# First batch's token mixing with the height tiles outermost, its weights decoded in pairs, and the second batch's attention written behind it

## The chip, the cores and the metric

One core of one Trainium2 chip. The metric is the device time of one execution in microseconds; the kernel before took 1106.73 us (median of 3 runs, 1104.41 to 1109.35). Engines: PE (TensorE, matrix products into eight PSUM banks), DVE (VectorE), ACT (ScalarE), POOL (GpSimd), SP (issues most of the DMAs, in order).

## The reference

Eight batches of 576 tokens and 512 channels go through linear attention and two mixer layers. Per batch:

```
kv  = k^T v per head;  x = rmsnorm(q kv) * g_norm        # 8 heads of 64
th  = x @ w_theta;  zr, zi = x*cos(th), x*sin(th)
y   = w_tok_r @ zr + w_tok_i @ zi                         # token mixing, 576 x 576 each
u   = x + y;  x2 = u + relu(u @ w_ch)                     # channel mixing
u2  = x2 + (relu(x2^T w_tok1) w_tok2)^T                   # second layer: tokens (256) ...
out = u2 + relu(u2 @ w_ch1) @ w_ch2                       # ... and channels (1536)
```

The mixer weights arrive as float64, so the kernel itself turns their two 32 bit words into float32 and those into a float16 pair.

## The kernel before

Each product of precision is made of three float16 matmuls (`mm3`): high by high, high by low, low by high. So every operand, weight or activation, exists as a pair of tiles, made by one ACT instruction (high) and one DVE instruction (low). A float64 weight tile costs more: ACT scales the upper word (L148), DVE shifts it (L154), ors in the lower word (L155) and the sign (L156), ACT makes the high half (L176), DVE the low one (L178).

A batch goes through these units, each a generator whose steps are run one by one:

- `kv` (L295): key by value sums, then the block diagonal `kvbd` (ACT L309, DVE L310), one buffer for all batches.
- `attend` r = 0 to 4 (L316): `po` = q by kvbd for 128 tokens (64 in the last), square (ACT L335), sum (DVE L337), inverse root (POOL L338, L339), x (DVE L342). Batch 0 transposes x on PE (`px`, L350; pair by L67, L68). Later batches make the pair xs (ACT L357, DVE L359) and transpose it by DMA (L360); R, the residual, follows (L363, L365).
- `rotate` r = 0 to 4: `pt` = the angles; L393 to L405 turn them into x cos and x sin (tile cs, two buffers), and L409, L412 write the pair zh, zl at the height tiles r and r + 4. The last one, r = 4 (64 tokens, cos and sin as one ninth height tile), works transposed and brings its tile zt to zh by a DMA transpose (L457). zt has the tag xs, which has two buffers, with batch 1's xs.
- `mix` (L462): for a chunk c of output tokens (256 or 320 columns) and a block dt of 128 channels, one accumulation over all nine height tiles kk in one PSUM bank; then the residual (DVE L483) and the pair u (ACT L484, DVE L487).
- `channel`, `token1`, `token2`: the layers that follow, with evictions at L509 to L517, L72 and L552.

Around them stands a planner: the code is written unit by unit, and the tile framework orders the instructions of each engine by the place where they are written and by when buffers and inputs are free in its own model of time. What is written later runs earlier where its inputs and buffers are there. Blocks marked `urgent` count as written 120 instructions earlier.

The start (L768 to L790) does kv and attend of batch 0, with a mixing weight tile after each (`spare`), then its rotations with the rest of those tiles, then loads batch 1's heads and does its kv. Nine raw weight tiles come by DMA into buffers that the z tiles will use: pairs of adjacent tiles in tag zh, single ones in tag zl, two buffers each. `prepare` names batch 0's own zh and zl; they get a buffer at their first write. Then the loop over b begins (L828): for b = 0 `run` does the eight mix blocks M00 to M13, each followed by a unit of batch 1 (a0 to a4, r0 to r2), then eight channel blocks with r3 and r4 and the w_tok weights; `l` loads a later batch's heads. For b = 1 the first four mix blocks are followed by token mixing of batch 0's second layer, beside which batch 2's attention starts.

PSUM is one pool of eight banks (`bank`), taken in turn by whatever is written.

Of the kernel before, what the change touches and what calls it, by code (L numbers as in the profile page):

```python
# [19 lines left out]
P = 128  # L20
# [8 lines left out]
def attn_mixer_kernel(  # L29
# [17 lines left out]
    HP = H // 2  # L47
    CHUNKS = ((0, 2 * P), (2 * P, S))
    NC = S // 2
    KH, MH, DH = KF // 2, KD // 2, KD // 2  # L50
    ps = ctx.enter_context(tc.tile_pool(name="ps", bufs=8, space=PSUM))
    dr = ctx.enter_context(tc.tile_pool(name="dr", bufs=1, space=DRAM))
# [23 lines left out]
    def lead(ins):  # L76

        last[ins.ins.engine] = ins.ins
        return ins
# [78 lines left out]
    def weight(pool, w, src, part, n, hi, lo, scale, name, raw=None):  # L158

        if pool is stg:  # L160
            val = pool.tile([P, n], F32, tag="val", name=f"{name}v")[:part]
        else:
            val = pool.tile([P, 8, P], F32, tag="st", name=f"{name}v").rearrange("p x n -> p (x n)")[:part, :n]
        if w.dtype == F32:
            load(val, src)
            yield
        else:
            if raw is None:
                raw = pool.tile([P, 4, P, 2] if pool is not stg else [P, n, 2], I32, tag="raw", name=f"{name}r")
                if pool is not stg:  # L170
                    raw = raw.rearrange("p a n w -> p (a n) w")
                raw = raw[:part, :n]
                load(raw.rearrange("p n w -> p (n w)"), src)
            yield
            yield from decode(val, raw)
        nc.scalar.activation(hi, val, AF.Copy, scale=scale)  # L176
        yield
        nc.vector.scalar_tensor_tensor(lo, val, scale, hi, ALU.mult, ALU.subtract)  # L178

    def words(w):  # L180
        return (w, 1) if w.dtype == F32 else (w.bitcast(I32), 2)

    def weight_tile(pool, w, pr, j, n, scale, name, col=0, raw=None):
        at = slice(col, col + n)
        src, k = words(w)
        src = src[j * P:(j + 1) * P, k * col:k * (col + n)]
        return weight(pool, w, src, P, n, pr[0][:, j, at], pr[1][:, j, at], scale, f"{name}{col}_{j}", raw)

    def mix_weights():

        if w_mix.dtype == F32:
            return [weight_tile(stg, w_mix, wm, j, S, SW, "wm") for j in range(KM)]
        units = []
        for j in range(KM):
            if j % 3 == 2:
                t, n = zp.tile([P, KM - 1, DM], F16, tag="zl", name=f"wmr{j}"), 1
            elif j % 3 == 0:
                t, n = zp.tile([P, KM + 1, DM], F16, tag="zh", name=f"wmr{j}"), 2
            else:
                continue  # L200
            t = t.rearrange("p a b -> p (a b)").bitcast(I32)[:, :n * 2 * S]
            src = w_mix.bitcast(I32)[j * P:(j + n) * P, :].rearrange("(k p) n -> p k n", p=P)
            nc.sync.dma_start(t.rearrange("p (k n) -> p k n", k=n), src)
            t = t.rearrange("p (k n w) -> p k n w", k=n, w=2)
            units += [weight_tile(stg, w_mix, wm, j + k, S, SW, "wm", raw=t[:, k]) for k in range(n)]
        return units


    wad = [dr.tile([P, KH, DH, 7, P], F16, name=f"wad{i}") for i in range(2)]
# [160 lines left out]
    def prepare(o):  # L370
        if o.zh is None:

            o.zh = zp.tile([P, KM + 1, DM], F16, tag="zh", name=f"zh{o.b}")
            o.zl = zp.tile([P, KM - 1, DM], F16, tag="zl", name=f"zl{o.b}")

    def rotate(o, r):

        b = o.b
        if r == 0:
            prepare(o)  # L380
        zh, zl, x, xt = o.zh, o.zl, o.x[r], o.xt[r]
        if r == NR:
            yield from rotate_last(o, xt)
            return
        pt = bank(f"pt{b}{r}")
        mm3(pt, [(xt[:, 0, kk, :], xt[:, 1, kk, :], wth[:, kk, :], wtl[:, kk, :]) for kk in range(KD)])

        cs = fp.tile([P, 2, DM], F32, tag="cs", name=f"cs{b}{r}", bufs=2)
        f, sn = cs[:, 0], cs[:, 1]
        place = beside(o)  # L390
        yield
        with early(o):
            place(nc.scalar.activation(f, pt, AF.Copy, bias=MAGIC))  # L393
        if b > 1:
            yield
        with early(o):
            place(nc.vector.scalar_tensor_tensor(f, f, MAGIC, pt, ALU.subtract, ALU.subtract))
        yield
        with early(o):
            place(nc.scalar.activation(sn, f, AF.Sin, scale=-RAD))  # L400
            nc.scalar.activation(f, f, AF.Abs)
            nc.scalar.activation(f, f, AF.Sin, bias=hpi, scale=-RAD)
        yield
        with early(o):
            place(nc.vector.tensor_tensor(cs, cs, x.unsqueeze(1).to_broadcast([P, 2, DM]), ALU.mult))  # L405
        yield
        at = slice(r, r + NR + 1, NR)
        with early(o):
            place(nc.scalar.activation(zh[:, at, :], cs, AF.Copy))  # L409
        yield  # L410
        with early(o):
            place(nc.vector.tensor_tensor(zl[:, at, :], cs, zh[:, at, :], ALU.subtract))  # L412

    def rotate_last(o, xt):


        b = o.b
        pt = bank(f"pt{b}{NR}")[:, :KD * SR].rearrange("p (k t) -> p k t", k=KD)
        for dt in range(KD):
            ds = slice(dt * P, (dt + 1) * P)  # L420
            mm3(pt[:, dt, :], [(wth[:, kk, ds], wtl[:, kk, ds], xt[:, 0, kk, :SR], xt[:, 1, kk, :SR]) for kk in range(KD)])
        cs = fp.tile([P, 2, DM], F32, tag="cs", name=f"cs{b}{NR}", bufs=2)
        f = cs[:, 0, :KD * SR].rearrange("p (k t) -> p k t", k=KD)
        sn = cs[:, 1, :].rearrange("p (k i t) -> p k i t", k=KD, i=2)
        zt = fp.tile([P, 2, DM], F16, tag="xs", name=f"zt{b}", bufs=2)
        place = beside(o)
        yield
        with early(o):
            place(nc.scalar.activation(f, pt, AF.Copy, bias=MAGIC))
        if b > 1:  # L430
            yield
        with early(o):
            place(nc.vector.scalar_tensor_tensor(f, f, MAGIC, pt, ALU.subtract, ALU.subtract))
        yield
        with early(o):
            place(nc.scalar.activation(sn[:, :, 1, :], f, AF.Sin, scale=-RAD))
            nc.scalar.activation(f, f, AF.Abs)
            nc.scalar.activation(sn[:, :, 0, :], f, AF.Sin, bias=hpi, scale=-RAD)
        if b > 1:
            yield  # L440
        R = o.R[:, :, SM:]
        with early(o):
            for i in range(2):
                place(nc.vector.scalar_tensor_tensor(sn[:, :, i, :], R, 1.0 / SW, sn[:, :, i, :], ALU.mult, ALU.mult))
            place(nc.scalar.activation(R, R, AF.Copy, scale=gn))
        yield
        sn = sn.rearrange("p k i t -> p (k i t)")
        with early(o):
            place(nc.scalar.activation(zt[:, 0, :], sn, AF.Copy))
        yield  # L450
        with early(o):
            place(nc.vector.tensor_tensor(zt[:, 1, :], sn, zt[:, 0, :], ALU.subtract))
        if b > 1:

            for _ in range(3):
                yield
        place(nc.sync.dma_start_transpose(  # L457
            o.zh[:, KM - 1:, :].rearrange("p i (k d) -> p (i k) d", k=KD), zt.rearrange("p i n -> p (i n)")
        ))


    def mix(o, c, dt):  # L462
# [22 lines left out]
        yield  # L485
        with urgent():
            lead(nc.vector.scalar_tensor_tensor(ul[:, dt, :], u, 1.0 / SW, uh[:, dt, :], ALU.mult, ALU.subtract))  # L487

    def channel(o, c, ct):
        b, R = o.b, o.R  # L490
# [249 lines left out]
    def go(unit, lead=False):  # L740
        advance()
        next(unit)
        (leading if lead else pending).append(unit)
# [16 lines left out]
    def spare(n=1):  # L760
        for _ in range(min(n, len(extra))):
            go(extra.pop(0))
# [10 lines left out]
    load_q(o, P)  # L773
    for part in range(2):
        go(kv(o, part))
    go(attend(o, 0))
    prepare(o)
    extra += mix_weights()
    for r in range(1, NR + 1):
        go(attend(o, r))  # L780
        spare()
    for r in range(NR + 1):
        go(rotate(o, r))
        if r > 1:
            spare()
    spare(len(extra))
    nxt = load_heads(1)
    for part in range(2):
        go(kv(nxt, part))
    flush()  # L790
    extra += [weight_tile(stg, w_ch, wc, j, DM, SW, "wc") for j in range(KD)]

# [35 lines left out]
    for b in range(B):  # L828
        loaded.clear()
        if b == 0:  # L830
            run(MIX, o, nxt, None, {
                "M00": "a0 w", "M01": "a1 w", "M02": "a2 w", "M03": "a3 w", "M10": "a4 r0 w", "M11": "r1 l w", "M12": "r2 w", "M13": "w",
            })
            after = loaded[0]
            spare(len(extra))
            flush()
# [5 lines left out]
            extra += [weight(wp[0], w_tok1, src[SM:], SR, DT, w1rh[:SR], w1rl[:SR], SW, "w1r")]  # L842
            extra += [weight_tile(wp[0], w_tok2, w2, j, S // 2, SW, "w2", col) for j in range(KJ) for col in range(0, S, S // 2)]
            run(CHANNEL, o, nxt, after, {
                "C00": "w", "C01": "r3 w", "C02": "w", "C03": "r4 w", "C10": "w", "C11": "w", "C12": "w", "C13": "w",
            })
            spare(len(extra))
            for t in (w1rh, w1rl):
# [95 lines left out]
```

## Time and profile before

| | |
|---|---|
| runs | 1104.41, 1106.73, 1109.35 us |
| profiled execution | 1103.0 us, its span 1101.2 us, granted clock 0.994 |
| busy over the span | PE 97%, DVE 74%, ACT 51%, POOL 17% |
| PE, tenths of the first four slices of 27.5 us | 4, 7, 7, 9 |
| DVE, the same | 4, 9, 8, 9 |
| granted PE clock, the same | 9, 9, 8, 9 |
| DMA in the first slice | 311 GB/s |
| chain that ended last | PE 86%, DVE 7%, DMA 3% |
| POOL inverse root (L339), mean of 40 | 1720 ns |
| ACT square (L335) and xs (L357), means | 583 and 622 ns |

Busy is the share of time in which an engine worked on something. A slice is one of 40 equal parts of the span, and its digit is in tenths. For an engine's cost per instruction the step from one start to the next is read where instructions stand back to back, since their durations overlap a little. Times in the rows are us from the start of the span.

### The profile page before, as it was taken

Reading aid. Unit: us, or ns where it says so; the run is one execution under the profiler, and the core shown is the slowest. Engines: PE = TensorE matmul, PEld = TensorE weight load, DVE = VectorE, ACT = ScalarE, POOL = GpSimd, SP = SyncE. Lnnn points to the kernel's source line nnn. Section 1 sums busy time; section 2 is a strip of 40 time slices with the busy share of each in tenths; the row PEclk is TensorE's granted clock in tenths of the full one; section 3 lists DMA queues with packets and bytes.
Section 4 is the critical chain, followed back from the end, with each engine's and each line's share of the span. In section 5 each row is a group of like instructions: output and inputs, shape, how many; then the busy total and the mean of one; then the engine's idle time right before and its main releaser. Section 6 shows DMA issues by size and latency. Waiting matters only on the chain.

```text
span 1101.2 us, 21603 instructions
## 1 busy us (share of the span) xinstructions
PE 1066.4 (97%) x8884; PEld 813.7 (74%) x8884; DVE 812.7 (74%) x1475; ACT 565.7 (51%) x966; POOL 186.7 (17%) x252
## 2 busy tenths in 40 slices
PE   4779999999999999999999999999999999999998
PEld 4466776767777678776877777777777777777776
DVE  4989868887988869877654685758586775758484
ACT  3857536556465654646431645446363645446360
POOL 2250032442814518243001000000000000000000
PEclk9989999999999999999999999999999999999999
DMA  9725675867748668472456402020201102020101
GB/s 311 263 69 144 139 193 130 227 156 186 230 107 222 172 165 242 96 175 69 102 205 202 162 23 65 11 76 2 85 3 39 50 22 66 12 76 1 44 1 44
DMA packets 146626, 126.31 MB, mean 115 GB/s; under 512 B 93216, under 2 KB 123040, under 8 KB 146528
## 3 DMA queue, kind: packets, MB, share of 16 engines
q1 hardware_dynamic: 141152, 104.49, 35.1%
q0 software_dynamic: 5376, 20.45, 5.1%
q8 instruction: 69, 1.13, 0.4%
q14 instruction: 29, 0.24, 0.1%
HBM read 74.25 MB, written 29.88 MB: 95 GB/s over the span
## 4 chain that ended last, share of the span: by engine, by line
PE 86%; DVE 7%; DMA 3%; ACT 1%; issue 1%; SPq 1%; POOL 0%; ACTq 0%; DVEq 0%
PE py L104 5%; PE py L105 5%; PE py L103 5%; PE na L103 4%; PE na L105 4%; PE pa L105 4%; PE pa L104 4%; PE pa L103 4%; PE na L104 4%; PE po L324 3%; PE pr L103 2%; PE pr L104 2%; PE pr L105 2%; PE pt L104 2%; PE nc L105 2%; PE nc L103 2%
## 5 line engine op out<-in xcount | busy, mean ns | idle before, releaser
L103 PE MATMUL py<-wmh,zh 128*128 128x256 f16 (+1 forms) x576 | 165.5, 288 | 3.9 <-DMA zh<-zt 2.4
L104 PE MATMUL py<-wml,zh 128*128 128x256 f16 (+1 forms) x576 | 165.4, 288 | 0.0
L105 PE MATMUL py<-wmh,zl 128*128 128x320 f16 (+1 forms) x512 | 146.4, 287 | 0.0
L105 PE MATMUL na<-gh,wbl 128*128 128x288 f16 x384 | 109.3, 286 | 0.0
L104 PE MATMUL pa<-o,wah 128*128 128x288 f16 x384 | 109.2, 286 | 0.0
L104 PE MATMUL na<-gl,wbh 128*128 128x288 f16 x384 | 109.1, 286 | 0.0
L103 PE MATMUL pa<-o,wah 128*128 128x288 f16 x384 | 108.4, 286 | 0.0
L105 PE MATMUL pa<-o,wal 128*128 128x288 f16 x384 | 107.8, 286 | 0.0
L103 PE MATMUL na<-gh,wbh 128*128 128x288 f16 x384 | 106.0, 286 | 0.2
L625 DVE TENSOR_TENSOR gl<-sum,gh 128x1152 f16<-128x1152 f32 x48 | 65.0, 1354 | 21.9 <-ACT gh L624 21.9
L104 PEld LDWEIGHTS <-wbh 128*128 128x128 f16 x672 | 65.7, 98 | 17.7 <-issue 1.0
L104 PEld LDWEIGHTS <-wah 128*128 128x128 f16 x672 | 65.8, 98 | 16.6
L103 PEld LDWEIGHTS <-wah 128*128 128x128 f16 x672 | 65.8, 98 | 16.6
L103 PEld LDWEIGHTS <-wbh 128*128 128x128 f16 x672 | 65.7, 98 | 16.6
L105 PEld LDWEIGHTS <-wal 128*128 128x128 f16 x672 | 65.8, 98 | 16.6
L105 PEld LDWEIGHTS <-wbl 128*128 128x128 f16 x672 | 65.7, 98 | 16.6
L105 PE MATMUL pr<-uh,wcl 128*128 128x256 f16 (+1 forms) x256 | 73.1, 286 | 0.0
L104 PE MATMUL pr<-ul,wch 128*128 128x256 f16 (+1 forms) x256 | 73.1, 286 | 0.0
L103 PE MATMUL pr<-uh,wch 128*128 128x256 f16 (+1 forms) x256 | 73.0, 286 | 0.0
L103 PEld LDWEIGHTS <-zh 128*128 128x128 f16 x576 | 56.7, 98 | 19.8 <-DMA zh<-zt 2.6
L339 POOL TENSOR_TENSOR ri<-ss,mhalf 128x8 f32<-128x8 f32 x40 | 68.8, 1720 | 2.5
L624 ACT ACTIVATE gh<-sum 128x1152 f16<-128x1152 f32 x48 | 55.5, 1156 | 25.6 <-DVE sum L672 25.6
(297 smaller groups left out, 2855.1 us busy)
## 6 DMA issues: line engine op xcount, KB each, us to landing
c<-u2d SPq DMA_DIRECT2D x32, 288.0 KB, 4.3
out<-c SPq DMA_DIRECT2D x64, 144.0 KB, 1.8
q<-in_q SPq DMA_DIRECT2D x7, 1152.0 KB, 6.5
k<-in_k SPq DMA_DIRECT2D x24, 256.0 KB, 5.6
v<-in_v SPq DMA_DIRECT2D x24, 256.0 KB, 5.7
wa_r<-in_w_ch SPq DMA_DIRECT2D x24, 256.0 KB, 4.1
wb_r<-in_w_ch SPq DMA_DIRECT2D x24, 256.0 KB, 4.4
wad<-wa POOLq DMA_DIRECT2D x24, 224.0 KB, 4.0
```

Of the source, the lines that this page charges most:

```text
L103: nc.tensor.matmul(acc, ah, bh, start=first and i == 0, stop=False, **more)
L104: nc.tensor.matmul(acc, ah, bl, start=False, stop=False, **more)
L105: nc.tensor.matmul(acc, al, bh, start=False, stop=last and i == n - 1, **more)
L324: nc.tensor.matmul(po[:, hp * P:(hp + 1) * P], o.q[:, hp, r * P:(r + 1) * P], kvbd[:, hp, :], start=True, stop=True)
L339: nc.gpsimd.tensor_tensor(ri, ss, mhalf, ALU.pow)
L624: nc.scalar.activation(h.hi[:, 3:], h.s, AF.Copy)
L625: nc.vector.tensor_tensor(h.lo[:, 3:], h.s, h.hi[:, 3:], ALU.subtract)
```

## The change

Batch 0's token mixing is done by `outer`: for one rotation r, both its height tiles (r and r + 4) are multiplied into six accumulations at once: all four channel blocks of the first chunk, two to a bank, and the first two blocks of the second chunk, one bank each. The four banks are held from the first of these units (X0) to the evictions behind the last (X3). M12 and M13, the other two accumulations, stay as they were, behind them. The order of the rotations is 0, 1, 4, 2, 3, and so is that of the sums (X4 stands ahead of X2). The weights are decoded two height tiles at a time, j and j + 4, from one load each; pair 1's raw words lie in a buffer of R, the ninth tile's in the staging pool. Rotations 2 and 3 take their cs from a spare zl buffer. Batch 1's heads are loaded ahead of all this; its attention is written beside M12 and M13, its rotations beside the channel blocks.

```diff
     def weight(pool, w, src, part, n, hi, lo, scale, name, raw=None):
-            val = pool.tile([P, n], F32, tag="val", name=f"{name}v")[:part]
+            val = pool.tile([P, n], F32, tag="val", name=f"{name}v", bufs=2)[:part]
+    def mix_pair(j, raw, m):
+        k = words(w_mix)[1]
+        at = slice(j, j + NR + 1, NR) if m == 2 else slice(j, j + 1)
...
+        nc.sync.dma_start(raw, src)
+        return mix_weight(j, raw, m, at)
+    def mix_weight(j, raw, m, at):
+        hi, lo = (t[:, at] for t in wm)
+        yield
...
+            val = stg.tile([P, 2, S], F32, tag="val", name=f"wm{j}v", bufs=2)[:, :m]
+            yield from decode(val, raw.rearrange("p i (n w) -> p i n w", w=2))
+        nc.scalar.activation(hi, val, AF.Copy, scale=SW)
+        yield
+        nc.vector.scalar_tensor_tensor(lo, val, SW, hi, ALU.mult, ALU.subtract)
     def mix_weights():
-        for j in range(KM):
-            if j % 3 == 2:
-                t, n = zp.tile([P, KM - 1, DM], F16, tag="zl", name=f"wmr{j}"), 1
-            elif j % 3 == 0:
-                t, n = zp.tile([P, KM + 1, DM], F16, tag="zh", name=f"wmr{j}"), 2
...
+        return [
+            mix_pair(0, zh(0), 2),
+            mix_pair(1, flat(mp.tile([P, KD, S], F32, tag="R", name="wmr1", bufs=2)), 2),
+            mix_pair(KM - 1, stg.tile([P, S, 2], I32, tag="raw", name=f"wmr{KM - 1}").rearrange("p n w -> p (n w)"), 1),
+            mix_pair(2, zh(2), 2),
+            mix_pair(3, zh(3), 2),
+        ]
+    spare_cs = []
+    def turned(b, r):
+        if b or r not in (2, 3):
+            return fp.tile([P, 2, DM], F32, tag="cs", name=f"cs{b}{r}", bufs=2)
+        if not spare_cs:
+            t = zp.tile([P, KM - 1, DM], F16, tag="zl", name="cs0").rearrange("p a b -> p (a b)").bitcast(F32)
+            spare_cs.extend([t[:, :2 * DM], t[:, 2 * DM:4 * DM]])
+        return spare_cs.pop(0).rearrange("p (i n) -> p i n", i=2)
+    def outer(o, r):
+        b, R, kks = o.b, o.R, (r, r + NR) if r < NR else (KM - 1,)
+        if r == ORDER[0]:
+            o.pa = [bank(f"pa{b}{i}").rearrange("p (i n) -> p i n", i=2) for i in range(2)]
+            o.pb = [bank(f"pb{b}{i}")[:, :NB] for i in range(2)]
+        cols = [slice(*c) for c in CHUNKS]
+        for kk in kks:
+            for dt in range(KD):
...
+                for c, acc in enumerate((o.pa[dt // 2][:, dt % 2], o.pb[dt] if dt < 2 else None)):
...
+                    mm3(acc, [part], first=first and (c == 1 or dt % 2 == 0), last=last, skip_group_check=True)
+        yield
+        if r != ORDER[-1]:
+            return
...
+        for c, dts, acc in parts:
+            u = R[:, dts, cols[c]]
+            with urgent():
+                lead(nc.vector.scalar_tensor_tensor(u, acc, gn, u, ALU.mult, ALU.add))
+                lead(nc.scalar.activation(o.u[c][0][:, dts], u, AF.Copy, scale=1.0 / SW))
...
-    go(attend(o, 0))
     prepare(o)
     extra += mix_weights()
-    for r in range(1, NR + 1):
-        go(attend(o, r))
-        spare()
-    for r in range(NR + 1):
-        go(rotate(o, r))
-        if r > 1:
+    nxt = load_heads(1)
+    for what in "a0 a1 a4 a2 w a3 r0 r1 r4 w r2 X0 r3 X1 w w w X4 X2 k X3 .".split():
+        if what == ".":
+            advance()
+        elif what == "w":
             spare()
-    spare(len(extra))
-    nxt = load_heads(1)
-    for part in range(2):
-        go(kv(nxt, part))
+        elif what == "k":
+            for part in range(2):
+                go(kv(nxt, part))
+        else:
+            go({"a": attend, "r": rotate, "X": outer}[what[0]](o, int(what[1])))
-            run(MIX, o, nxt, None, {
-                "M00": "a0 w", "M01": "a1 w", "M02": "a2 w", "M03": "a3 w", "M10": "a4 r0 w", "M11": "r1 l w", "M12": "r2 w", "M13": "w",
-            })
+            run(MIX[6:], o, nxt, None, {"M12": "a0 w a1 w l", "M13": "a2 w a3 w"})
             run(CHANNEL, o, nxt, after, {
-                "C00": "w", "C01": "r3 w", "C02": "w", "C03": "r4 w", "C10": "w", "C11": "w", "C12": "w", "C13": "w",
+                "C00": "a4 w r0", "C01": "r1 w", "C02": "r2 w", "C03": "r3 w", "C10": "r4 w", "C11": "w", "C12": "w", "C13": "w",
             })
```

## Rows read from the trace of the kernel before

**Rows 1.** Stretches: length, busy time (instructions) by engine, PE clock, DMA share, GB/s.
```profile
core 0: us, PE busy (x) PEld busy (x) DVE busy (x) ACT busy (x) POOL busy (x), PEclk, DMA share, GB/s
27.00:50.00 23.00, 17.38 (x177) 10.98 (x175) 22.86 (x38) 20.11 (x34) 6.80 (x7) 1.00 0.71 262
50.00:84.00 34.00, 25.44 (x204) 21.05 (x201) 28.71 (x45) 19.63 (x34) 14.01 (x8) 0.85 0.35 106
84.00:121.30 37.30, 37.30 (x285) 24.94 (x283) 35.81 (x68) 29.19 (x58) 2.06 (x2) 0.95 0.52 128
121.30:144.00 22.70, 21.89 (x224) 16.05 (x222) 17.95 (x50) 9.68 (x23) 0.00 (x0) 1.00 0.68 171
144.00:1101.20 957.20, 952.25 (x7898) 729.90 (x7898) 694.61 (x1257) 477.60 (x805) 158.48 (x220) 1.00 0.38 104
```

**Rows 2.** Waits of DVE, 27 to 144 us: total, times, longest.
```profile
DVE xs L359 <- ACT xs L357: 3.5, 1, 3.5
DVE x L342 <- POOL ri L339: 1.8, 1, 1.8
DVE w2l L178 <- ACT w2h L176: 1.5, 3, 0.5
```

**Rows 3.** Timeline, all engines, 79 to 84 us: start, duration, what, idle before.
```profile
80.00 1.37 SPq L457 DMA_TRANSPOSE zh<-zt  x1
...
83.42 0.28 PE L103 MATMUL py<-wmh,zh 128*128 128x256 f16 x1 [2.38 <-DMA zh<-zt]
...
83.45 0.63 ACT L357 ACTIVATE xs<-x 128x512 f16<-128x512 f32 x1 [5.41 <-DMA zh<-zt]
```

**Rows 4.** Timeline of DVE, 27 to 29 and 718 to 721 us.
```profile
27.51 0.76 DVE L155 SCALAR_TENSOR_TENSOR wm_0v<-wmr,wm_0v 128x576 int32<-128x576 int32 x1
28.18 0.46 DVE L154 TENSOR_SCALAR wm_1v<-wm_1v 128x576 int32<-128x576 int32 x1
28.57 0.68 DVE L342 TENSOR_TENSOR x<-po,ri 128x512 f32<-128x512 f32 x1
...
718.83 1.35 DVE L600 SCALAR_TENSOR_TENSOR o<-t,o 128x1152 f16<-128x1152 f32 x1
720.10 0.45 DVE L684 SCALAR_TENSOR_TENSOR c<-na,c 128x288 f32<-128x288 f32 x1
```

**Rows 5.** Timeline of PE, 70 to 72 us, a mixing block's matmuls.
```profile
70.83 0.27 PE L103 MATMUL py<-wmh,zh 128*128 128x256 f16 x1
70.94 0.27 PE L104 MATMUL py<-wml,zh 128*128 128x256 f16 x1
...
71.05 0.30 PE L103 MATMUL py<-wmh,zh 128*128 128x320 f16 x1
71.19 0.30 PE L104 MATMUL py<-wml,zh 128*128 128x320 f16 x1
```

**Rows 6.** Timeline of DVE and ACT, 47 to 49 us.
```profile
47.23 0.75 DVE L156 SCALAR_TENSOR_TENSOR wm_4v<-wmr,wm_4v 128x576 int32<-128x576 int32 x1
...
48.01 1.06 ACT L409 ACTIVATE zh<-cs 128x1024 f16<-128x1024 f32 x1
```

**Rows 7.** Groups of DVE instructions, 27 to 144 us: busy us, mean ns, idle before.
```profile
L412 DVE TENSOR_TENSOR zl<-cs,zh 128x1024 f16<-128x1024 f32 x8 | 9.7, 1219 | 0.3 <-ACT zh L409 0.3
L405 DVE TENSOR_TENSOR cs<-cs,x 128x1024 f32<-128x1024 f32 x8 | 9.7, 1217 | 0.2 <-ACT cs L402 0.2
```

**Rows 8.** Timeline of PE: batch 1's first and fourth po.
```profile
55.91 0.58 PE L324 MATMUL po<-kvbd,q 128*128 128x128 f32 x1 [0.69 <-DVE kvbd L310]
...
67.26 0.58 PE L324 MATMUL po<-kvbd,q 128*128 128x128 f32 x1 [1.88 <-DVE x L342]
```

**Rows 9.** SP's queue: a load of batch 1's heads, its transposes, zt1's transpose.
```profile
18.50 0.38 SPq L272 DMA_DIRECT2D k<-in_k  x1
...
81.47 1.27 SPq L360 DMA_TRANSPOSE xt<-xs  x1
...
87.85 11.83 SPq L360 DMA_TRANSPOSE xt<-xs  x3
...
122.97 1.24 SPq L457 DMA_TRANSPOSE zh<-zt  x1
```

More of the change, by code (lines that the diff above doesn't have):

```diff
@@ L49, in attn_mixer_kernel @@
     NC = S // 2
+    NB = S - 2 * P
+    ORDER = (0, 1, NR, 2, 3)
     KH, MH, DH = KF // 2, KD // 2, KD // 2
@@ L168, in weight @@
             if raw is None:
-                raw = pool.tile([P, 4, P, 2] if pool is not stg else [P, n, 2], I32, tag="raw", name=f"{name}r")
+                raw = pool.tile([P, 4, P, 2] if pool is not stg else [P, S, 2], I32, tag="raw", name=f"{name}r")
                 if pool is not stg:
@@ L187, in weight_tile @@
         return weight(pool, w, src, P, n, pr[0][:, j, at], pr[1][:, j, at], scale, f"{name}{col}_{j}", raw)
-    def mix_weights():
-        if w_mix.dtype == F32:
-            return [weight_tile(stg, w_mix, wm, j, S, SW, "wm") for j in range(KM)]
-        units = []
-        for j in range(KM):
-            if j % 3 == 2:
-                t, n = zp.tile([P, KM - 1, DM], F16, tag="zl", name=f"wmr{j}"), 1
-            elif j % 3 == 0:
-                t, n = zp.tile([P, KM + 1, DM], F16, tag="zh", name=f"wmr{j}"), 2
[L199 to L206, printed above, removed]
+    def mix_pair(j, raw, m):
+        k = words(w_mix)[1]
+        at = slice(j, j + NR + 1, NR) if m == 2 else slice(j, j + 1)
+        raw = raw[:, :m * S * k].rearrange("p (i n) -> p i n", i=m)
+        src = w_mix if k == 1 else w_mix.bitcast(I32)
+        src = src[:2 * SM].rearrange("(i r) n -> r i n", i=2)[j * P:(j + 1) * P] if m == 2 else src[j * P:(j + 1) * P].unsqueeze(1)
+        if k == 1:
+            raw = raw.bitcast(F32)
+        nc.sync.dma_start(raw, src)
+        return mix_weight(j, raw, m, at)
@@ new lines, in mix_weight, with flat, zh @@
+    def mix_weight(j, raw, m, at):
+        hi, lo = (t[:, at] for t in wm)
+        yield
+        if w_mix.dtype == F32:
+            val = raw
+        else:
[4 more added lines that the diff above has]
+        nc.vector.scalar_tensor_tensor(lo, val, SW, hi, ALU.mult, ALU.subtract)
+    def mix_weights():
+        def flat(t):
+            return t.rearrange("p a b -> p (a b)").bitcast(I32)
+        def zh(j):
+            return flat(zp.tile([P, KM + 1, DM], F16, tag="zh", name=f"wmr{j}"))
+        return [
[5 more added lines that the diff above has]
+        ]
@@ L386, in rotate @@
         mm3(pt, [(xt[:, 0, kk, :], xt[:, 1, kk, :], wth[:, kk, :], wtl[:, kk, :]) for kk in range(KD)])
-        cs = fp.tile([P, 2, DM], F32, tag="cs", name=f"cs{b}{r}", bufs=2)
+        cs = turned(b, r)
         f, sn = cs[:, 0], cs[:, 1]
@@ L421, in rotate_last @@
             mm3(pt[:, dt, :], [(wth[:, kk, ds], wtl[:, kk, ds], xt[:, 0, kk, :SR], xt[:, 1, kk, :SR]) for kk in range(KD)])
-        cs = fp.tile([P, 2, DM], F32, tag="cs", name=f"cs{b}{NR}", bufs=2)
+        cs = turned(b, NR)
         f = cs[:, 0, :KD * SR].rearrange("p (k t) -> p k t", k=KD)
@@ L487, in mix @@
             lead(nc.vector.scalar_tensor_tensor(ul[:, dt, :], u, 1.0 / SW, uh[:, dt, :], ALU.mult, ALU.subtract))
+    def outer(o, r):
[6 more added lines that the diff above has]
+            for dt in range(KD):
+                ds = slice(dt * P, (dt + 1) * P)
+                low = o.zl[:, kk, ds] if kk < KM - 1 else o.zh[:, KM, ds]
+                first, last = kk == ORDER[0], r == ORDER[-1] and kk == kks[-1]
+                for c, acc in enumerate((o.pa[dt // 2][:, dt % 2], o.pb[dt] if dt < 2 else None)):
+                    if acc is None:
+                        continue
+                    part = (o.zh[:, kk, ds], low, wm[0][:, kk, cols[c]], wm[1][:, kk, cols[c]])
+                    mm3(acc, [part], first=first and (c == 1 or dt % 2 == 0), last=last, skip_group_check=True)
+        yield
+        if r != ORDER[-1]:
+            return
+        o.u = []
+        for c, n in enumerate((2 * P, NB)):
+            o.u.append(tuple(mp.tile([P, KD, n], F16, tag=f"{k}{c}", name=f"{k}{b}{c}") for k in ("uh", "ul")))
+        parts = [(0, slice(2 * i, 2 * i + 2), acc) for i, acc in enumerate(o.pa)] + [(1, slice(i, i + 1), acc.unsqueeze(1)) for i, acc in enumerate(o.pb)]
+        for c, dts, acc in parts:
[3 more added lines that the diff above has]
+                lead(nc.scalar.activation(o.u[c][0][:, dts], u, AF.Copy, scale=1.0 / SW))
+        yield
+        for c, dts, acc in parts:
+            with urgent():
+                lead(nc.vector.scalar_tensor_tensor(o.u[c][1][:, dts], R[:, dts, cols[c]], 1.0 / SW, o.u[c][0][:, dts], ALU.mult, ALU.subtract))
     def channel(o, c, ct):
@@ L775, in attn_mixer_kernel @@
         go(kv(o, part))
-    go(attend(o, 0))
     prepare(o)
     extra += mix_weights()
-    for r in range(1, NR + 1):
-        go(attend(o, r))
-        spare()
-    for r in range(NR + 1):
-        go(rotate(o, r))
-        if r > 1:
-            spare()
-    spare(len(extra))
-    nxt = load_heads(1)
-    for part in range(2):
-        go(kv(nxt, part))
+    nxt = load_heads(1)
[3 more added lines that the diff above has]
+        elif what == "w":
+            spare()
+        elif what == "k":
+            for part in range(2):
+                go(kv(nxt, part))
+        else:
+            go({"a": attend, "r": rotate, "X": outer}[what[0]](o, int(what[1])))
     flush()
```

## The prediction

> **What bounds the kernel now.** I read the table of stretches first [rows 1]. From 144 us to the end PE (TensorE) is busy 952.25 of 957.2 us, and the change touches none of that work. Between 27 and 144 us PE is busy 17.38 + 25.44 + 37.30 + 21.89 = 102.0 of 117 us, so it idles 15.0; two of the stretches also show a granted clock of 0.85 and 0.95, worth up to 0.15 x 34 + 0.05 x 37.3 = 7.0 us. VectorE (DVE) is busy 22.86 + 28.71 + 35.81 + 17.95 = 105.3 us there, idle 11.7. So the startup is DVE's: it feeds PE with decoded weights and split tiles. It has to get through its list before token mixing of batch 0 and attention of batch 2 go on at 144, whatever the order of the list. A new order can win only where DVE stands still, or where the list gets shorter.
>
> Next, DVE's waits, to see where it stands still [rows 2]: 3.5 us before L359, 1.8 before L342, the rest in waits of up to 1.2 us on ACT's half of a decode or split. The 3.5 is one event, seen in the timeline [rows 3]: the transpose of zt0, the last tile of batch 0's rotations, is issued only at 80.00. Until it has landed, PE waits 2.38 us with the mixing's ninth height tile, and ACT 5.41 us for a buffer in which the next xs of batch 1 is to go (tag xs has two, zt is one of its tenants). Behind that ACT wait DVE has nothing left.
>
> **The change part by part.** I count DVE's list from 27 to the 144 mark as 117 us = 105.3 of work + 11.7 idle.
>
> *Pairs.* Four pairs of weight tiles with four DVE instructions each: 16 instructions fewer. Back to back, a 576 column pass takes 0.67 us to the next start, the shift before it 0.39, a 1152 column pass 1.27 [rows 4]. Three passes save 3 x (2 x 0.67 - 1.27) = 0.2 a pair, 0.8 in all; the shift I leave at twice its price. In the evictions two instructions of 512 columns take the place of four of 256, for the sum and for the low part: four fewer, at the same 0.07 each 0.3. Together 1.1 us off the list. Bounds: 0, and 20 instructions at 0.09 (what a 576 column pass shows as busy, 0.76, over its step) = 1.8.
>
> The Trainium skill asks more for an instruction: its page "VectorE: DVE Perf Modes", section "Walkthrough: the 8-slice pipeline in each mode", has some 150 cycles of init and decode beside the elements. At the page's 0.96 GHz 20 instructions would save 3.1 us, an estimate by that page, and the time would come out 2 us earlier; these rows show 0.07 between back-to-back instructions.
>
> *PE's work.* The same matmuls in another order, no columns more or less. Per height tile the sums take 12 matmuls of 256 columns and 6 of 320, at 0.11 and 0.135 a start [rows 5]: 2.1 us, nine tiles 19. The two accumulations left as they were (M12, M13) take 27 x 0.135 = 3.6 each.
>
> *The rotations in the order 0, 1, 4, 2, 3.* zt0 is no longer the last tile; its transpose lies beside the decode and the mixing of other tiles. The event of rows 3 goes, DVE's 3.5 and PE's 2.38. Late next is batch 1's x behind POOL's power, the 1.8 of rows 2. I leave 1.0 of the 5.3 idle in 50 to 84.
>
> *When the sums start.* The z tile has the tag zh with two buffers, which raw weights use first. In before ACT's first write of it (L409, 48.01) starts as DVE's last read of wm_4's raw words ends (47.23 + 0.75) [rows 6]: it waited for that buffer. After the change pairs 0 and 2 take both and pair 3 the first one freed, so z comes behind pair 2's decode. DVE's list to there: 11 attention instructions left of batch 0 (0.6 each, 6.6), pairs 0 and 1 (0.78 + 3 x 1.27 each, 9.2), four times L397 and L405 (0.6 + 1.15, 7.0), the ninth tile (2.4), pair 2 but its low part (3.3) = 28.5, from 27 to 55. With L409 and L412 (1.06 and 1.22) [rows 6, 7] the sums start near 57.5. Their 19 us, some 2 of waiting for zt0 (whose cs buffer is freed by rotation 0's L412) and some half clock bring them to 80, M12 and M13 to 87. I cost this late start at nothing, because DVE meanwhile has zl, the rest of the decode and batch 1's first instructions to do; the cover is gone where batch 1's attention isn't there yet (last rival).
>
> *Batch 1's attention.* It is written later, but the planner already runs what is written late as soon as its inputs are there: batch 1's first po ran at 55.91, amid batch 0's mixing [rows 8]. I expect that again. The loads of batch 1's heads now stand ahead of the loop, six of 256 KB and q on SP's queue, which is in order, ahead of pair 3's. In before the first of them went out at 18.50 amid the weights [rows 9]. Bounds: 0, and the 5 us in which 1.57 MB pass at the page's 311 GB/s, if DVE has to wait for all of it; I take 0.4, nearer to the row, since pair 3 waits for a buffer in any case.
>
> *The w_tok decodes* keep their place behind the channel blocks; some 2 us of them that before had done by 121 come later now. The 4.75 us of idle after 121.3 are hand-overs with ACT, 0.5 at a time [rows 2]; with a denser list I leave 3.5.
>
> *Sum.* Idle left: 0.5 (27 to 50, was 0.14) + 1.0 (was 5.29) + 1.7 (was 1.49) + 3.5 (was 4.75) = 6.7 of 11.7. The gain is 11.7 - 6.7 + 1.1 = 6.1 us. PE permits it: its 102 us could end at 129. The profiled execution took 1103.0 us around its span of 1101.2, so 1096.9; the median of the runs shown, 1106.73, lies 3.7 above it, and on that scale it is **1100.6 us**. Bounds of the idle: 2 us (hand-overs alone) gives 1095.9, 11.7 (each wait returns elsewhere) 1105.6.
>
> **The rivals.**
> *DVE hardly waits.* Idle of 1 to 3 us: 1095 to 1097. For it: PE has room, 15 us idle and the clock [rows 1]. Against: the hand-overs [rows 2] are in the code unchanged.
>
> *The bubble moves, or the change doesn't do what it says.* The sums start late for want of a buffer, at 57 where before's first mixing came with its first z tile at 48 to 50 [rows 6]; and batch 1's five xs still share two buffers with zt1. The three transposes behind the first two held SP for 11.83 us from 87.85 [rows 9]. With batch 0 out of the way less lies beside them, and the 11.7 us of idle come back there: 1105.6, no change.
>
> *Batch 1's chain becomes the bound (slower).* Place: the four banks that hold the sums. In before batch 1's fourth po waited 1.88 us for DVE's L342, which frees a bank [rows 8], with fewer sums open. If four are held from 57 to 80 and the rest goes to pt and kvp, batch 1's po runs where it is written, behind the first late accumulation, at 84. From its po to its first transpose six instructions of 0.6 to 0.7 and POOL's power (1.7) pass, 6 us: 90, against 81.47 in before [rows 9]. From there to zt1's transpose at 122.97 it was 41.5 us; unchanged, all of it comes 8.5 us later: 1115. It decides from the moment that the first transpose passes 81.5. The Trainium skill speaks for this rival: "Perfetto Trace Analysis", section "Optimizing Tensor Performance", wants independent matmul groups to rotate through the banks, so that evictions overlap the next group; the wait of 1.88 us agrees.
>
> **How the numbers follow.** About 0.5%, 5.5 us, is what can be told from no change: faster is under 1101.2, slower over 1112.3. The forecast (1097 to 1104) has 0.46, of which 0.36 lies under 1101.2; DVE hardly waiting 0.14; the bubble moving 0.20; the chain 0.20. Faster 0.36 + 0.14 = 0.50, same 0.10 + 0.20 = 0.30, slower 0.20. The range runs from 1093, a little below no idle at all (1106.7 - 11.7 - 1.1 = 1093.9), to 1112, where most of the chain's case is left out; the forecast's own is 1097 to 1104.
>
> **What would show it.** Right: no ACT wait of 5 us for zt's buffer; 6 to 7 us of DVE idle from 27 us to the kvbd copy before batch 2's po; that copy near 138, in before at 144; first sums near 57; batch 1's po ahead of the sums' end; batch 1's mixing from 113 to 116 on. Wrong: DVE idle for several us behind 80, with L342 or L359 of batch 1 after it; a first transpose of batch 1 behind 85; or, the other way, sums that start before 50, which would say that z got a buffer first. PE idle that grows behind 144 would void the frame of the argument.

## The result, and the profile after

The change made the kernel slower: 1116.29 us, the median of 6 runs (1113.48 to 1117.39), against 1106.61 before; the ratio is 1.0082, 95% interval 1.0067 to 1.0098. The forecast was 1100.6. The profiled execution took 1116.65 us, its span 1114.9, granted clock 0.988. Line numbers below are those of the changed kernel. Two of the ten runs of the last experiment, kernel 12 (1132.83 and 3954.20 us), were slow ones and are left out of its time.

First the table of stretches, columns as in [rows 1].

```profile
27.00:50.00 23.00, 13.84 (x106) 7.37 (x104) 21.98 (x28) 17.66 (x27) 8.37 (x7) 0.88 0.67 251
50.00:84.00 34.00, 29.82 (x275) 21.99 (x276) 22.87 (x27) 16.66 (x26) 0.00 (x0) 0.88 0.37 101
84.00:121.30 37.30, 30.62 (x204) 19.49 (x203) 31.68 (x53) 24.03 (x45) 9.78 (x10) 0.91 0.49 120
121.30:144.00 22.70, 22.70 (x235) 17.27 (x231) 17.82 (x45) 12.30 (x26) 0.00 (x0) 1.00 0.66 149
144.00:155.40 11.40, 5.45 (x57) 3.00 (x55) 9.38 (x25) 5.82 (x15) 0.00 (x0) 0.92 0.78 203
27.00:155.40 128.40, 102.43 (x867) 69.14 (x865) 103.74 (x175) 76.46 (x136) 18.14 (x17) 0.91 0.54 151
155.40:1114.90 959.50, 955.02 (x7900) 732.02 (x7900) 697.51 (x1260) 477.38 (x806) 158.01 (x220) 1.00 0.37 103
```

The mark, batch 2's first po, stood at 144.52 us before and stands at 155.40: 10.9 of the 13.7 us by which the profiled span is longer. (The medians differ by 9.7; the execution profiled before was 3.6 us faster than its median.) From the mark on the two take 956.7 and 959.5 us. Up to it DVE has 103.7 us of work in 128.4: 24.7 us idle, where before it had 105.8 in 117.5, 11.7 idle. So the work up to the mark got 2.0 us shorter and the idle time 12.9 longer. Most of the new idle time lies from 50 to 84, 11.1 us where [rows 1] had 5.3, and from 84 to 121.3, 5.6 where before there were 1.5. DVE's waits (columns as in [rows 2]) show what it stood for:

```profile
DVE wc_0v L156 <- ACT wc_0v L150: 8.5, 1, 8.5
DVE w_3v L156 <- ACT w_3v L150: 4.0, 1, 4.0
DVE R L389 <- ACT R L387: 1.7, 2, 1.2
```

The 8.5 us are one event, at 70.7, named after a decode that was next in the list. ACT had waited as long, for the raw words of wc_0. SP's queue (start, duration, what) says why they came so late:

```profile
34.18 0.37 SPq L200 DMA_DIRECT2D wmr<-in_w_mix  x1
68.36 0.33 SPq L296 DMA_DIRECT2D k<-in_k  x1
...
72.18 0.42 SPq L143 DMA_DIRECT2D wc_0r<-in_w_ch  x1
...
94.93 1.24 SPq L384 DMA_TRANSPOSE xt<-xs  x1
```

For 34 us SP stood at one load, the fourth row of batch 1's k, which needs a buffer that kvp reads; wc_0 is queued behind it. The last row is batch 1's first transposed xs, at 81.47 before [rows 9]. PE's timeline has what both go back to:

```profile
54.18 0.39 PE L105 MATMUL pa<-wmh,zh 128*128 128x256 f16 x1 [9.53 <-ACT zh L444]
...
59.76 0.56 PE L328 MATMUL kvp<-v,k 128*64 128x64 f32 x10
...
67.88 1.38 PE L328 MATMUL kvp<-v,k 128*64 128x64 f32 x38
...
79.02 1.15 PE L328 MATMUL kvp<-v,k 96*64 96x64 f32 x32
...
85.25 2.05 PE L348 MATMUL po<-kvbd,q 128*128 128x128 f32 x16 [0.32 <-DVE kvbd L334]
```

The sums start at 54.18 after 9.5 us of nothing, kvp is strewn among them, and batch 1's first po runs at 85.25, when the sums are through (their last matmul starts at 84.25). In [rows 8] it ran at 55.91. No ACT wait for zt's buffer is left, so the bubble of [rows 3] is gone.

### The profile page after: what moved, and what is told of

Its sections match the earlier page's. It is cut to its first block, busy times and chain, and to the rows that moved or that the text cites. A ratio compares the mean times of both kernels' runs of the same rounds, so it can differ in the third digit from the quotient of the medians.

```text
span 1114.9 us, 21575 instructions
## 1 busy us (share of the span) xinstructions
PE 1070.0 (96%) x8884; PEld 812.4 (73%) x8884; DVE 814.1 (73%) x1455; ACT 564.0 (51%) x956; POOL 181.7 (16%) x252
## 4 chain that ended last, share of the span: by engine, by line
PE 85%; DVE 5%; DMA 5%; ACT 3%; SPq 1%; issue 1%; POOL 0%; ACTq 0%
PE py L107 5%; PE py L106 5%; PE py L105 5%; PE na L105 4%; PE na L107 4%; PE pa L106 4%; PE pa L107 4%; PE pa L105 4%; PE na L106 4%; PE po L348 3%; PE pt L107 3%; PE pt L105 3%; PE pt L106 2%; PE nc L107 2%; PE nc L105 2%; PE pc L107 2%
## 5 line engine op out<-in xcount | busy, mean ns | idle before, releaser
L105 PE MATMUL py<-wmh,zh 128*128 128x320 f16 (+1 forms) x522 | 149.3, 286 | 1.4 <-DMA zh<-zt 1.4
L106 PE MATMUL py<-wml,zh 128*128 128x320 f16 (+1 forms) x522 | 149.3, 286 | 0.0
L107 PE MATMUL py<-wmh,zl 128*128 128x320 f16 (+1 forms) x464 | 132.3, 286 | 0.0
L693 ACT ACTIVATE gh<-sum 128x1152 f16<-128x1152 f32 x48 | 55.5, 1156 | 25.5 <-DVE sum L741 25.5
```

The costliest lines, as they stand in the source:

```text
L105: nc.tensor.matmul(acc, ah, bh, start=first and i == 0, stop=False, **more)
L106: nc.tensor.matmul(acc, ah, bl, start=False, stop=False, **more)
L107: nc.tensor.matmul(acc, al, bh, start=False, stop=last and i == n - 1, **more)
L693: nc.scalar.activation(h.hi[:, 3:], h.s, AF.Copy)
```

## The experiments

Two theories. A: batch 1's kv is written behind the sums, so kvp, po and all that DVE does with them come too late. B: the sums start late because z waits for pair 2's raw words. C in the expectations: the four held banks keep po behind the sums. Within A it stayed open whether the loss lies in SP's queue or in po's place on PE; later the banks got runs of their own. Times are medians, and all ratios are to the kernel before, run beside each.

| kernel | us | ratio (95%) | mark | DVE work, idle to it | batch 1's po from |
|---|---|---|---|---|---|
| before | 1106.6 to 1107.3 | 1 | 144.52 | 105.8, 11.7 | 55.9 |
| after | 1116.29 | 1.0082 (1.0067 to 1.0098) | 155.40 | 103.7, 24.7 | 85.3 |
| 1 after, kv ahead of the sums | 1103.58 | 0.9973 (0.9962 to 0.9985) | 144.29 | 103.0, 14.3 | 68.7 |
| 2 after, k and v in own buffers | 1115.33 | 1.0078 (1.0063 to 1.0093) | 153.15 | 103.2, 23.0 | 84.5 |
| 3 after, wc loaded first | 1118.38 | 1.0101 (1.0081 to 1.0120) | 153.77 | 102.9, 23.8 | 86.6 |
| 4 after, z not waiting | 1110.86 | 1.0038 (1.0023 to 1.0053) | 148.92 | 102.9, 19.0 | 70.9 |
| 5 = 1, two banks held | 1104.54 | 0.9975 (0.9963 to 0.9987) | 143.98 | 104.5, 12.5 | 60.6 |
| 6 = 1, z not waiting | 1106.08 | 0.9993 (0.9979 to 1.0006) | 143.06 | 102.5, 13.5 | 61.0 |
| 7 = 5 and 6 together | 1100.76 | 0.9934 (0.9919 to 0.9949) | 141.21 | 104.3, 9.9 | 61.8 |
| 8 = 7, units earlier | 1103.24 | 0.9965 (0.9953 to 0.9978) | 142.12 | 103.6, 11.6 | 57.1 |
| 9 after, no outermost tiles | 1103.51 | 0.9961 (0.9945 to 0.9976) | 143.13 | 106.7, 9.5 | 55.5 |
| 10 = 9, z not waiting | 1105.06 | 0.9982 (0.9970 to 0.9993) | 143.66 | 105.6, 11.0 | 57.3 |
| 11 = 9, order 0 to 4, no spare cs | 1110.08 | 1.0032 (1.0019 to 1.0045) | 148.45 | 103.6, 17.9 | 54.9 |
| 12 before, order 0, 1, 4, 2, 3 | 1105.44 | 0.9981 (0.9968 to 0.9995) | 145.32 | 105.7, 12.7 | 55.4 |

Work and idle time are us of the profiled execution, from 27 to the mark. In every row the work lies within 4.2 us; idle time has a range of 15. These columns are of one execution each, up to 2.7 us from the kernel's median (before: 3.6), so marks 2 or 3 us apart tell little by themselves.

**1. kv ahead of the sums.**

```diff
-    for what in "a0 a1 a4 a2 w a3 r0 r1 r4 w r2 X0 r3 X1 w w w X4 X2 k X3 .".split():
+    for what in "a0 a1 a4 a2 w a3 r0 r1 r4 w r2 k X0 r3 X1 w w w X4 X2 X3 .".split():
```

> The changed kernel with one word moved in its written order: batch 1's key-value sums (k) ahead of X0 instead of behind X2. Theory A, the late key-value sums: in the changed kernel they stand on PE behind the first token sums (59.8 to 80.2 us); the loads of batch 1's last k and v rows wait for them on SP's queue until 68.4, the w_ch loads stand behind those, and DVE has nothing to do from 70.7 to 79.2. By A the sums run in PE's gap near 45, w_ch is there by 58, DVE's wait of 8.5 us goes, batch 1's first po comes before 75 instead of 85.25, and the time falls by 7 to 11 us to 1105 to 1109. Rival B, the z tile that gets its buffer late (first sums at 54 after a PE wait of 9.5 us): that wait stays, and the time with it, 1114 to 1118. Rival C, the four banks: po stays behind the sums, 1114 to 1118.

It fell by 12 us, more than expected, to 1103.58, faster than before. The place of one letter in the list is the whole loss and more. wc_0's load went out at 43.87 us, and two po (8 matmuls each) ran from 68.74 on, though the sums ended later than in the changed kernel (last matmul at 87.4). The other three po ran behind the sums:

```profile
68.74 0.38 PE L348 MATMUL po<-kvbd,q 128*128 128x128 f32 x2
...
69.23 1.50 PE L348 MATMUL po<-kvbd,q 128*128 128x128 f32 x12
...
70.70 0.38 PE L348 MATMUL po<-kvbd,q 128*128 128x128 f32 x2
...
88.83 1.95 PE L348 MATMUL po<-kvbd,q 128*128 128x128 f32 x16
```

**2. SP's queue or po's place?** Batch 1's last k and v rows get buffers of their own.

```diff
-        pool, bufs = (kp, 2) if b == 0 and r > 2 else (fp, 3)
+        pool, bufs = (kp, 2) if b <= 1 and r > 2 else (fp, 3)
-        for r in range(3 if b else NR + 1):
+        for r in range(3 if b > 1 else NR + 1):
```

> The changed kernel with buffers of their own for batch 1's last k and v rows, so that their loads don't wait for batch 1's first key-value sums; the written order is unchanged. A says which part SP's queue has: the rows' loads go out near 30, w_ch is no longer behind them and arrives before 75 instead of 78.5, so some of DVE's wait of 8.5 us goes, but the key-value sums stay behind the first four height tiles on PE and po comes near 75 to 80: 1109 to 1113. If SP's queue were the whole of it, 1106. B and C: no change, 1114 to 1118.

A miss: 1115.33, no change. The edit was to free SP's queue and didn't: the next load, batch 2's k, stood there until 68.45, and wc_0 went out at 70.77. But the trace answers another part. DVE copied kvbd 14 us earlier, at 70.73 in place of 84.77, and the first po still ran at 84.52.

**3. The same question without that flaw.** The loads of wc_0 and wc_1 are written ahead of the sums.

```diff
-    for what in "a0 a1 a4 a2 w a3 r0 r1 r4 w r2 X0 r3 X1 w w w X4 X2 k X3 .".split():
+    for what in "a0 a1 a4 a2 w a3 r0 r1 r4 w r2 c X0 r3 X1 w w w X4 X2 k X3 .".split():
+        elif what == "c":
+            ahead = [weight_tile(stg, w_ch, wc, j, DM, SW, "wc") for j in range(2)]
+            for g in ahead:
+                next(g)
-    extra += [weight_tile(stg, w_ch, wc, j, DM, SW, "wc") for j in range(KD)]
+    extra += ahead + [weight_tile(stg, w_ch, wc, j, DM, SW, "wc") for j in range(2, KD)]
```

> The changed kernel with one edit: the loads of the first two w_ch tiles are written ahead of the sums, so that they stand on SP's queue ahead of batch 1's k load, which waits until 68 us. kv, po and the sums stay where they are. DVE's wait of 8.5 us for wc_0 goes in any case. If po's place on PE, behind the sums, is the loss (first po still at 84 to 86, first transposed xs behind 90): 1113 to 1116, no gain, the idle time comes back behind the sums. If the loads that stood behind the k load are a loss of their own: 1107 to 1111.

No gain: 1118.38, somewhat above its first case. wc_0 went out at 33.80 and its wait is gone. DVE's timeline shows what stands there instead:

```profile
74.28 0.43 DVE L334 COPY kvbd<-kvp 64x256 f32<-64x256 f32 x1 [1.37 <-ACT kvbd L333]
84.97 0.55 DVE L551 SCALAR_TENSOR_TENSOR R<-pb,gn,R 128x320 f32<-128x320 f32 x1 [10.27 <-PE pb L107]
```

It waits 10.3 us for the sums' end. kvbd was complete at 74.7, yet PE went on with the sums and took po at 86.57. So while po stands behind the sums, wc_0's long stay in SP's queue costs nothing by itself: it only gave the idle time its name. The loss is po's place in PE's order. Why po stands there although kvbd is ready isn't settled by kernels 2 and 3: the planner's own estimate of when kvbd is there, or want of a bank (C), would look the same.

**4. z not waiting** (in the changed kernel; pair 2's raw words get a buffer of their own).

```diff
-            mix_pair(2, zh(2), 2),
+            mix_pair(2, stg.tile([P, 2 * S, 2], I32, tag="raw2", name="wmr2", bufs=1).rearrange("p n w -> p (n w)"), 2),
```

> The changed kernel with a buffer of its own for the raw words of pair 2, so that z's tile has one when its first write is ready. B: the first token sums start near 46 instead of 54, everything behind them moves up by 8, and the time falls by 6 to 9 us to 1107 to 1110. A: the key-value sums stand behind the sums on PE and come up with them, by 8 us at most, but DVE's decode is not done earlier, so the wait for batch 1 shifts only partly: 1110 to 1114. C: no change.

The sums began at 49.04, and the time fell by some 5 us to 1110.86, still slower than before and within A's range. B is a part, but not by an earlier end: the sums' last matmul started at 86.23, later than in the changed kernel. The key-value sums came up with the first sums, kvbd was copied at 69.50 in place of 84.77, and two po ran amid the sums:

```profile
70.89 1.95 PE L348 MATMUL po<-kvbd,q 128*128 128x128 f32 x16
...
86.23 0.27 PE L107 MATMUL pa<-wmh,zl 128*128 128x256 f16 x1
```

Four banks were held here too, so these alone don't keep the first two po back. Why kernel 2, with kvbd 1.2 us later than here, doesn't let them through stays open.

**5 to 7. Banks and z, each alone and together**, on the kernel with kv ahead. "Two banks" drops the second chunk's blocks from the sums (`pb`); M10 and M11 follow as M12 and M13 do.

```diff
-            o.pb = [bank(f"pb{b}{i}")[:, :NB] for i in range(2)]
-            run(MIX[6:], o, nxt, None, {"M12": "a0 w a1 w l", "M13": "a2 w a3 w"})
+            run(MIX[4:], o, nxt, None, {"M10": "a0 w", "M11": "a1 w", "M12": "a2 w l", "M13": "a3 w"})
```

> The kernel with batch 1's kv ahead of the sums, and in it only the first chunk's two banks are held; all four accumulations of the second chunk follow behind the sums. Bank theory: in the kernel with kv ahead the third po of batch 1 came only at 88.8 us, behind the evictions of the held banks; with two banks it comes before 76, PE's wait of 4 us for the transposed xs at batch 1's rotations goes, and the time falls from 1103.6 to 1100 to 1102. Rival (DVE's list sets the end of the startup and the banks are no matter): within 1.5 us of 1103.6, whatever po does.

> The kernel with batch 1's kv ahead of the sums, and in it pair 2's raw words in a buffer of their own, so that z needs no buffer of theirs. If the late start of the sums (54.2 us in the changed kernel, 6.9 us of PE waiting with kv ahead) is still on the path that sets the end: 1098 to 1101. If kv's place was all of the loss and DVE hides the late start, as the prediction had it: 1102 to 1105, no different from the kernel with kv ahead.

> Both edits on the kernel with kv ahead: two banks held in place of four, and pair 2's raw words in a buffer of their own. If both are waits on the path, their gains add: 1096 to 1099, near the bound that DVE's list sets with hand-overs alone (1096). If they are two covers of one wait: no better than the better of the two alone.

The mechanism of the first expectation came, its gain didn't: the third po ran at 69.40 in place of 88.83, PE's wait for xt went, and the time is the same, as the rival had it. z alone brought nothing either (1106.08, a little above its second case): the mark came 1.2 us earlier, and from there to the end it took 962.6 us where kernel 1 took 957.8 (1.5 of it between 195 and 205 us, where PE is busy 7.79 us, and 9.24 in kernel 1). Together they bring 0.4% over kernel 1, intervals apart, and the fastest version of all: 1100.76. Neither case of the third expectation had this: the two do more than the better one alone, and less than 1099. Kernel 6's po, then kernel 7's:

```profile
61.02 1.72 PE L348 MATMUL po<-kvbd,q 128*128 128x128 f32 x14
...
62.85 0.38 PE L348 MATMUL po<-kvbd,q 128*128 128x128 f32 x2
...
87.51 1.95 PE L348 MATMUL po<-kvbd,q 128*128 128x128 f32 x16
```

```profile
61.84 1.05 PE L348 MATMUL po<-kvbd,q 128*128 128x128 f32 x8
...
63.55 1.05 PE L348 MATMUL po<-kvbd,q 128*128 128x128 f32 x8
...
65.25 1.05 PE L348 MATMUL po<-kvbd,q 128*128 128x128 f32 x8
...
90.81 1.05 PE L348 MATMUL po<-kvbd,q 128*128 128x128 f32 x8
```

With four banks held, the third po ran only behind the sums, whether they started at 55 (kernel 1) or at 49 (kernel 6); with two, a third po gets through. This edit does more than free banks: it also takes over a third of the columns out of the sums and moves batch 1's units to other blocks, and no run separates these. The rule that the Trainium skill's "Perfetto Trace Analysis" has in "Optimizing Tensor Performance", groups that rotate through the banks, agrees with these po's (65.25 against 87.51) as far as the banks are the reason, but in kernel 5 alone it was worth nothing. Kernel 7's stretches:

```profile
50.00:84.00 34.00, 29.75 (x202) 21.62 (x203) 32.44 (x43) 21.56 (x35) 7.99 (x6) 0.86 0.30 75
84.00:121.30 37.30, 37.30 (x314) 26.64 (x312) 35.27 (x72) 29.48 (x56) 3.82 (x4) 1.00 0.53 126
```

DVE idles 3.6 us in them, in the changed kernel 16.8. Why each edit alone gains nothing no single run shows.

**8. Units still earlier.**

```diff
-            run(MIX[4:], o, nxt, None, {"M10": "a0 w", "M11": "a1 w", "M12": "a2 w l", "M13": "a3 w"})
+            run(MIX[4:], o, nxt, None, {"M10": "a0 w a1 w", "M11": "a2 w a3 w", "M12": "a4 w l r0", "M13": "r1 w"})
```

> The best kernel so far (kv ahead, z not waiting for raw words, two banks held: 1100.8) with batch 1's attention units written one or two places earlier, beside M10 to M12 in place of M10 to M13, and its rotations from M12 on. There the fourth and fifth po ran only at 90.8 and 92.6 and the fourth transpose at 99.3. If batch 1's chain still sets the end of the startup: 1097 to 1100. If DVE's list does: 1100 to 1102.

A miss on both sides, 1103.24, intervals apart from kernel 7: the mark came 0.9 us later, and the rest took 1.5 us longer. Earlier isn't better without end; the last steps of such a list aren't settled by this theory.

**9 and 10. No outermost tiles**: the eight blocks of the kernel before, batch 1's units beside them, the rest of the change kept.

```diff
-    for what in "a0 a1 a4 a2 w a3 r0 r1 r4 w r2 X0 r3 X1 w w w X4 X2 k X3 .".split():
+    for what in "a0 a1 a4 a2 w a3 r0 r1 r4 w r2 w r3 w w k .".split():
-            run(MIX[6:], o, nxt, None, {"M12": "a0 w a1 w l", "M13": "a2 w a3 w"})
+            run(MIX, o, nxt, None, {
+                "M00": "a0 w", "M01": "a1 w", "M02": "a2 w", "M03": "a3 w", "M10": "a4 r0 w", "M11": "r1 l w", "M12": "r2 w", "M13": "w",
+            })
```

> The changed kernel with the height tiles' order undone: token mixing of batch 0 again as eight blocks M00 to M13, one bank each, with batch 1's attention beside them as in the kernel before; the weights in pairs, the order 0, 1, 4, 2, 3 of the rotations and the spare cs stay. If pairs and order bring what their terms say (1.1 us of shorter list, 1.4 us measured for the order alone in the kernel before): 1103 to 1105. If the outermost height tiles themselves are worth something, this is slower than the kernel with kv ahead (1103.6) by over 1 us; if they are worth nothing or cost, it is no slower.

> The kernel with the outermost height tiles undone (1103.5), and in it pair 2's raw words in a buffer of their own, as z's first buffer; PE waited 4.7 us for z there. If the earlier z is worth something only together with few banks held, it shows here too, since each block takes one bank in turn: 1099 to 1102. If the two held accumulations over all height tiles are what makes z's buffer pay: 1103 to 1104.

Kernel 9 is as fast as kernel 1, so the outermost tiles as changed bring nothing; held in two banks and with z free (kernel 7) they are worth some 0.3% over kernel 9, with intervals that just touch, and 0.5% over kernel 10, which has z free too, with intervals apart. In kernel 10 the early z doesn't pay, as its second case had it, though 1105.06 is a little above that case.

**11. Pairs without the order**: kernel 9 with the rotations 0 to 4 in order and no spare cs. Batch 1's heads are still loaded ahead, so besides the pairs this differs from the kernel before.

> The pairs alone: token mixing as in the kernel before, the rotations in the order 0 to 4, no spare cs; only the weights are decoded in pairs, from one load each. The prediction's term for the pairs is 1.1 us off DVE's list (0.8 of it in the decodes): 1105.5 to 1106.5 against 1107.3 before. By a fixed cost of some 150 cycles an instruction, 12 instructions fewer make 1.9 us: 1105 to 1105.5. If the pairs cost a buffer of z (first mixing later than 50 us) and that is on the path: 1108 to 1110.

1110.08, slower than before: the third case, at its upper end. (The expectation counts 12 instructions fewer; the trace has 16.) The mixing began at 54.66 (50.00 before), and the wait of [rows 2] was there again:

```profile
DVE xs L383 <- ACT xs L381: 3.6, 1, 3.6
```

**12. The order alone**, in the kernel before.

```diff
-    for r in range(1, NR + 1):
+    for r in (1, NR, 2, 3):
-    for r in range(NR + 1):
+    for i, r in enumerate((0, 1, NR, 2, 3)):
```

> The kernel before with one part of the change: attention and rotations of batch 0 in the order 0, 1, 4, 2, 3. The prediction said that the late zt0 costs DVE 3.5 and PE 2.4 us of idle; if that idle is worth its length, the time falls by 2 to 5 us below the kernel before, 1102 to 1105. Rival: DVE's list is the bound and the hole is filled from later work, so the idle moves: within 1.5 us of the kernel before.

0.2% faster, 1.8 us by the medians, between the two cases. From 50 to 84 DVE's idle time fell from 5.3 to 0.9 us, so the bubble went, but to the mark it is 12.7 in place of 11.7. Added to pairs (kernel 11 to kernel 9), order and spare cs are worth 0.7%; what share is the spare cs wasn't measured. Pairs and early heads without the order cost 0.3%. With it they no longer cost, and whether they pay isn't clear: 0.9961 for kernel 9 against 0.9981 for the order alone, intervals that overlap.

## Why the prediction was wrong

**The step that failed** is "Batch 1's attention": "the planner already runs what is written late as soon as its inputs are there ... I expect that again." It didn't hold. In the kernel before, kv of batch 1 was written ahead of all mixing, and only its attention late. The change moves kv itself behind X2. The prediction priced only the heads' loads, which move ahead (0.4 us); the move of kv it put at nothing, without naming it. Kernel 1 undoes it alone: 12 us. And inputs that are there don't suffice: in kernel 3 kvbd was complete 12 us before po ran. Why the planner kept po there stays open.

**"When the sums start"**: forecast 57.5, measured 54.18, for the reason given: ACT's z began at 53.07, as DVE's last pass over pair 2's words (51.69, 1.35 us) ended. (ACT itself came free just then, too; kernel 4, which gives these words another buffer, began its sums at 49.04.) Costed at nothing because DVE would have batch 1's first instructions to do meanwhile; that cover wasn't there, as the same sentence warned, and kernel 4 prices it at some 5 us. With the cover back (kernel 6) it is worth nothing, as costed, as long as four banks are held; with two (kernel 5 to kernel 7) it is worth 0.4%.

**Pairs**: the size of an instruction was right: in the changed kernel a 1152 column pass steps by 1.26 us, priced at 1.27:

```profile
29.04 1.35 DVE L157 SCALAR_TENSOR_TENSOR wm0v<-wmr,wm0v 128x1152 int32<-128x1152 int32 x1
30.30 0.68 DVE L70 SCALAR_TENSOR_TENSOR xt<-px,xt 128x512 f16<-128x512 f32 x1
```

That the list got 1.1 us shorter isn't shown: the work to the mark fell by 2.0, but five instructions of the w_tok2 decodes, 2.1 us, moved behind it. The fixed cost that the Trainium skill states in "VectorE: DVE Perf Modes", "Walkthrough: the 8-slice pipeline in each mode", showed no more here than in [rows 4], 0.07 us between two half passes and a whole one. What pairs do to buffers was left out of this term: without the order they lose 0.3% (kernel 11, with the heads loaded ahead).

**The rotations**: right in place and size from 50 to 84 (5.3 to 0.9 us, kernel 12), too high as a gain: 4.3 us were counted, and kernel 12 gained some 2. By its profile the idle time came back later, as the second rival said.

**The sum**: the frame held. PE's idle time behind the mark didn't grow (4.5 us, 4.4 before), and the time followed the mark. Where the forecast had 6.7 us of idle time, the changed kernel shows 24.7; kernel 1, with the failed step undone, 14.3; kernel 7 9.9. So that step isn't all: with it undone the gain is 0.3% where 0.6% was forecast.

**The third rival** is what happened, by its place and its size. Forecast: first po at 84, first transpose at 90, all behind it 8.5 later, 1115. Measured: 85.25, 94.93, the mark 10.9 later, 1116.29. Its sign, a first transpose behind 81.5, holds in the changed kernel and in kernels 2 to 4 (92.22, 94.67 and 82.36), and not in kernel 1 (78.52). Its cause was at most half right: it put po behind the sums because of held banks. The third po came forward when two banks were held in place of four (kernel 1 to 5, 6 to 7); the first two were held back by kv's place, and kernels 1 and 4 let them through with four banks held. So the rival's time was right partly by luck. It had 0.20. Looking for `k` in the start's list, behind X2, would have spoken for it.

## What to carry to other kernels

When a block is made long, list everything written behind it that an idle engine will need, the producers as well as the consumers: a consumer that can run early is no use if its producer has been moved back. When an engine waits, take away the wait that the profile names only after asking what it would do next; here that wait (8.5 us) came back as another (10.3 us). Edits that only pay together, such as early sums and fewer banks, are to be measured together too.

## What the runs showed of the hardware

After the 9.53 us gap PE came back slower. The stretches of the changed kernel around it:

```profile
44.65:54.18 9.53, 0.00 (x1) 0.00 (x1) 8.62 (x10) 6.82 (x10) 0.00 (x0) 0.67 0.01 2
54.18:58.10 3.92, 3.92 (x13) 1.94 (x14) 3.92 (x4) 2.70 (x4) 0.00 (x0) 0.50 0.00 0
58.10:60.00 1.90, 1.90 (x16) 0.83 (x15) 1.90 (x3) 1.16 (x1) 0.00 (x0) 1.00 0.00 0
```

The granted clock is 0.50, 1.2 GHz, for the 3.9 us from the sums' start on and 1.00, 2.4 GHz, right behind. A step of 512 columns is 0.43 us there (56.50 to 56.93) and 0.22 after (58.59 to 58.81):

```profile
56.50 0.63 PE L106 MATMUL pt<-wtl,xt 128*128 128x512 f16 x1
56.93 0.63 PE L107 MATMUL pt<-wth,xt 128*128 128x512 f16 x1
...
58.59 0.38 PE L106 MATMUL pt<-wtl,xt 128*128 128x512 f16 x1
58.81 0.38 PE L107 MATMUL pt<-wth,xt 128*128 128x512 f16 x1
```

By these steps the 3.9 us of work would have taken half as long at the higher clock: an estimate of some 2 us on PE beyond the gap's length, which the prediction had only as "some half clock".
